# A layer norm that reads PSUM, in a kernel whose instruction order is packed by a scheduler: identity matmuls for the residual, a shorter GpSimd chain, a split second DFT

## The chip, the cores and the metric

The kernel runs on one core of one Trainium2 chip. The metric is the device time in microseconds (us) of one execution; each kernel is executed several times and the median is quoted. The profile is one such execution; its span is about 2 us shorter than the time (290.0 against 291.84 for before). In this kernel TensorE multiplies matrices, VectorE and ScalarE do elementwise work, GpSimd does small things and starts bulk loads, SyncE starts stores and small transposing transfers. Two memories are named below: PSUM, whose banks (`bank` in the profile) this kernel's matmuls write, and SBUF, which holds its other tiles.

A run over 1.5% above the fastest of its kernel is called slow, the others fast. Verdicts here use fast runs alone, with 2% as the bound of "faster" and "slower", and compare each kernel with the kernel before on the same chip in the same rounds.

## The reference, cut to what matters

Four batches of sorted block attention (8 heads, 768 tokens, head size 64) give `x` of 768 x 512 for each batch. Then:

```python
X = np.fft.fft(x, axis=1); X = np.fft.fft(X, axis=2)
u = x + np.real(X)
mu = u.mean(-1); var = ((u - mu) ** 2).mean(-1)
un = (u - mu) / np.sqrt(var + 1e-06)
out = u + np.maximum(un @ w_ch1, 0.0) @ w_ch2      # 512 -> 2048 -> 512
```

The kernel does the two Fourier transforms as matmuls with constant matrices ("first DFT" over tokens, "second DFT" over the 512 columns). A batch has six tiles of 128 tokens in two groups of three: group (b, 0) and group (b, 1). An MLP step works on one group. TensorE's MLP work fills most of the time; the attention of batch 0 must come first.

## The kernel before: the parts that matter

Every operation is handed to a planner with an estimated cost. The planner simulates the engines and emits one fixed order of instructions for each engine:

```python
            for s in o.succs:                  # after operation o was placed
                s.left -= 1
                for x in s.costs:
                    s.ready[x] = max(s.ready[x],
                                     o.end + (0.03 if x == e else self.XL))
```

So one changed cost or dependency can reorder everything behind it. The second DFT and the layer norm (`rt` holds x; `RSC` undoes a scale):

```python
    many("u", 6, [128, DM], F32)          # six result buffers in all
    # ... in dft2(b, g), tiles 0 to 2:
    for c in range(4):
        nc.tensor.matmul(ps[:, o:o + 256], y[:, c, w0:w0 + 128], dtab[:, c, :], ...)
    nc.tensor.matmul(ps, lt[:, l0:l0 + 128], rb, start=False, stop=True)
    V.scalar_tensor_tensor(u, rt[:, T, :], RSC, ps, op0=ALU.mult, op1=ALU.add)
    V.bn_stats(st, u)
    V.bn_aggr(mv[:, tt, :], st)
    # ... once for each group, G is GpSimd:
    G.tensor_scalar(var, var, 1e-6, None, op0=ALU.add)
    G.tensor_tensor(ny, var, mhalf, op=ALU.pow)
    G.tensor_tensor(nm, mean, ny, op=ALU.mult)
    G.tensor_scalar(nm, nm, -1.0, None, op0=ALU.mult)
    # ... each tile, on ScalarE or VectorE:
    un = u * ny + nm
    # batch 0: transposed by TensorE, copied, then the MLP
```

The result is added to `u`, and `u` is stored. The q and k of batches 2 and 3 are loaded late, into a buffer (`kq`) whose last readers are on VectorE:

```python
    def load_qk(nm, b, hf, prio):
        after = lns[1:2] if b > 1 else ()
        # ... gpsimd.dma_start into kq[:, slot[nm, b, hf], :]
```

The softmax here doesn't subtract the row's maximum and nothing guards it: scores larger than these inputs give would overflow.

## Time and profile before

| | before |
|---|---|
| time, median of 3 runs (range), us | 292.2 (292.06 to 293.51) |
| profiled span, us | 290.0 |
| first second-DFT matmul / first MLP matmul, us | 58.45 / 70.25 |
| TensorE busy in 120 to 150 and in 150 to 277, us | 30.00 of 30, 126.89 of 127 |

The page's picture of the run cuts the span in 40 slices (7.25 us each). Slices are counted from 0. A digit is the busy share in tenths; `PEclk` is the granted TensorE clock in tenths.

```profile
PE   0389988897999999999999999999999999999980
DVE  4697999999999999831579643145034226210020
PEclk9997999998899999999999999999999999999997
```

TensorE (`PE`) is nearly full from slice 10 on. VectorE (`DVE`) is full in slices 4 to 15, so there it is VectorE that limits. The table of stretches gives, for each stretch, its length, the busy time of TensorE, of its weight loads, of VectorE, ScalarE and GpSimd, then the granted clock, the DMA share and GB/s:

```profile
67.50:70.90 3.40, 1.64 (x21) 1.04 (x18) 3.33 (x12) 1.84 (x3) 1.87 (x5) 1.00 0.02 5
70.90:74.30 3.40, 3.40 (x17) 2.06 (x16) 2.89 (x6) 2.31 (x5) 3.39 (x6) 0.50 0.45 48
120.00:150.00 30.00, 30.00 (x222) 16.39 (x220) 14.24 (x34) 15.35 (x34) 5.86 (x9) 1.00 0.18 50
```

In 67.5 to 70.9 TensorE works less than half of the time (1.64 of 3.4 us), and in the next 3.4 us its clock is 0.50. A stretch of 3.4 us, as long as this one at half clock, is called a window below. The layer norm of the first group lies just ahead of that. The timeline of VectorE (start, duration, engine, line, operation, output and input, count):

```profile
59.77 1.87 DVE L1160 SCALAR_TENSOR_TENSOR u<-rt,bank 128x512 f32<-128x512 f16 x3
61.56 1.28 DVE L1186 BATCH_NORM_STATS2 st<-u 128x6 f32<-128x512 f32 x2
...
66.21 0.55 DVE L1217 TENSOR_SCALAR un<-u,ny,nm 128x512 f16<-128x512 f32 x1
```

and of TensorE (in brackets: idle time ahead, and what ended it):

```profile
58.45 0.60 PE L1149 MATMUL bank<-vcx,y 128*128 128x256 f16 x4 [0.34 <-ACT ex L961]
...
66.94 0.38 PE L1232 MATMUL bank<-pack,un 128*128 128x128 f16 x4 [0.15 <-DVE u L1181]
...
70.25 2.13 PE L1253 MATMUL bank<-ut,w1sb 128*128 128x384 f16 x8 [0.67 <-ACT ut L660]
```

From the second DFT (L1149) to the first transposes (L1232) pass 8.5 us, and TensorE fills most of them with attention work of batch 1.

```profile
109.39 0.34 SPq L1287 DMA_DIRECT2D out_dram<-u  x1
109.91 4.70 SPq L915 DMA_TRANSPOSE qt<-kq  x3
115.70 0.33 SPq L1289 DMA_DIRECT2D out_dram<-u  x1
```

### The profile page before, as it was taken

The numbers are of one execution on the slowest core, as the hardware profiler recorded it, in microseconds if no ns is written. First come the engines' busy times: TensorE is split into PE (matmuls) and PEld (weight loads), VectorE is DVE, ScalarE is ACT, GpSimd is POOL, SyncE is SP. The second block draws the span as 40 slices with busy tenths as digits, with TensorE's granted clock in tenths as the row PEclk, the third lists the DMA queues.
The fourth block names the chain that finished last, engine by engine and source line by source line (L and its number), as shares of the span: only waits on it lengthen the run. The fifth ranks groups of instructions, "written<-read, shape, count | busy, mean of one in ns | idle before, by whom it ended". The sixth has DMA issues, their size and how long they took to land.

```text
span 290.0 us, 5807 instructions
## 1 busy us (share of the span) xinstructions
PE 260.9 (90%) x2284; PEld 155.2 (54%) x2284; DVE 171.9 (59%) x405; ACT 157.9 (54%) x323; POOL 66.3 (23%) x104
## 2 busy tenths in 40 slices
PE   0389988897999999999999999999999999999980
PEld 0258866554565656554566456455555546545530
DVE  4697999999999999831579643145034226210020
ACT  2677979785778945970477037137415505425300
POOL 8973300015900640011220002032000212200021
PEclk9997999998899999999999999999999999999997
DMA  7999999910990897211113010311311111221001
GB/s 114 211 260 245 215 208 211 219 37 5 157 146 10 95 165 133 66 37 20 77 47 57 36 52 22 58 72 50 57 72 37 38 54 72 38 90 36 2 36 72
DMA packets 42529, 26.33 MB, mean 91 GB/s; under 512 B 30106, under 2 KB 38824, under 8 KB 42500
## 3 DMA queue, kind: packets, MB, share of 16 engines
q0 software_dynamic: 23536, 18.31, 37.4%
q1 hardware_dynamic: 18966, 7.64, 11.6%
q8 instruction: 18, 0.29, 0.4%
q14 instruction: 9, 0.07, 0.1%
HBM read 28.96 MB, written 6.29 MB: 122 GB/s over the span
## 4 chain that ended last, share of the span: by engine, by line
PE 62%; DVE 22%; DMA 8%; issue 3%; POOL 2%; ACT 1%; POOLq 0%; DVEq 0%
PE bank L1253 26%; PE bank L1274 25%; DMA hr<-in_v_dram 4%; DVE vsf L660 3%; DVE vcx L708 3%; DVE rt L1006 3%; DMA out_dram<-u,rows 2%; POOL kq L472 2%; DMA kq<-in_q_dram 2%; PE bank L1149 2%; PE bank L991 2%; DVE st L1186 1%; PE bank L952 1%; PE bank L897 1%; DVE ks L660 1%
## 5 line engine op out<-in xcount | busy, mean ns | idle before, releaser
L1265 ACT ACTIVATE hr<-bank 128x384 f16<-128x384 f32 x115 | 56.3, 491 | 75.2 <-PE bank L1253 74.4
L1253 PE MATMUL bank<-ut,w1sb 128*128 128x384 f16 x512 | 92.8, 329 | 0.7 <-ACT ut L660 0.7
L1274 PE MATMUL bank<-w2sb,hr 128*128 128x512 f16 x384 | 87.9, 379 | 0.0
L1253 PEld LDWEIGHTS <-w1sb 128*128 128x128 f16 x512 | 49.0, 99 | 34.8 <-issue 1.8
L1274 PEld LDWEIGHTS <-hr 128*128 128x128 f16 x384 | 36.7, 98 | 41.8 <-issue 0.2
L1282 DVE TENSOR_TENSOR u<-bank,u 128x512 f32<-128x512 f32 x24 | 16.5, 689 | 60.2 <-PE bank L1274 59.8
L961 ACT ACTIVATE ex<-bank 96x384 f32<-96x384 f32 x64 | 27.9, 485 | 6.3 <-PE bank L952 6.0
L1295 POOL DMA_INDIRECT out_dram<-u,rows x12 | 12.2, 1013 | 77.0 <-DVE u L1282 56.7
L1193 POOL TENSOR_SCALAR mv<-mv 128x3 f32<-128x3 f32 x8 | 1.9, 240 | 109.8 <-DVE mv L1188 109.8
L976 ACT ACTIVATE eb<-ex,negone 96x384 f16<-96x384 f32 x35 | 20.8, 615 | 0.2
L1213 ACT ACTIVATE un<-u,nm,ny 128x512 f16<-128x512 f32 x15 | 12.2, 810 | 11.8 <-DMA ut<-un 8.5
L1172 DVE SCALAR_TENSOR_TENSOR u<-rt,bank 128x510 f32<-128x510 f16 x12 | 8.1, 678 | 16.3 <-PE bank L1138 8.9
L991 PE MATMUL bank<-vsf,eb 97*128 97x65 f16 x416 | 16.5, 193 | 1.3 <-DVE rr L836 0.5
L1006 DVE TENSOR_TENSOR rt<-bank,rz 128x384 f16<-128x384 f32 x32 | 17.2, 549 | 0.3
L991 PEld LDWEIGHTS <-eb 97*128 97x128 f16 x416 | 15.4, 98 | 3.6 <-issue 1.3
L472 POOL DMA_DIRECT2D kq<-in_q_dram x20 | 16.4, 850 | 1.7 <-DMA kq<-in_q_dram 1.2
L1186 DVE BATCH_NORM_STATS2 st<-u 128x6 f32<-128x512 f32 x24 | 16.1, 686 | 0.3
L1160 DVE SCALAR_TENSOR_TENSOR u<-rt,bank 128x512 f32<-128x512 f16 x12 | 8.0, 684 | 13.9 <-PE bank L1153 13.5
L927 PE MATMUL bank<-pack,qr 128*128 128x128 f16 x48 | 4.8, 246 | 12.3 <-ACT qr L660 11.7
L724 PE MATMUL bank<-bdv,vcx 128*128 128x128 f16 (+1 forms) x128 | 12.6, 225 | 0.0
L952 PE MATMUL bank<-qt,ks 64*128 64x96 f16 x256 | 11.3, 207 | 1.3 <-DVE rt L1006 0.4
L897 PE MATMUL bank<-bdk,kq 128*64 128x128 f16 x192 | 10.7, 228 | 1.6 <-DVE bdk L636 0.8
(130 smaller groups left out, 338.2 us busy)
## 6 DMA issues: line engine op xcount, KB each, us to landing
kq<-in_k_dram POOLq DMA_DIRECT2D x8, 384.0 KB, 6.6
w1sb<-in_moe_w_ch_dram POOLq DMA_DIRECT2D x4, 512.0 KB, 16.0
w2sb<-in_moe_w_ch_dram POOLq DMA_DIRECT2D x4, 512.0 KB, 19.0
out_dram<-u SPq DMA_DIRECT2D x8, 256.0 KB, 2.0
kq<-in_q_dram POOLq DMA_DIRECT2D x4, 384.0 KB, 11.6
hr<-in_v_dram POOLq DMA_DIRECT2D x2, 768.0 KB, 11.2
kq<-in_v_dram POOLq DMA_DIRECT2D x2, 768.0 KB, 21.5
kq<-in_q_dram POOLq DMA_DIRECT2D x16, 96.0 KB, 5.5
```

What stands on the lines that cost most here:

```text
L472: o = P.add({eng: c}, lambda _: e.dma_start(dst, src), r=r, w=w, prio=prio, nbytes=nbytes, tag="load", after=after)
L897: nc.tensor.matmul(ps.ap[64 * h2:64 * h2 + 64, 128 * r3:128 * r3 + 128], k16[:, 2 * hl + h2, 3 * half + r3, :], bdk[:, 2 * hp + h2].rearra ...
L952: nc.tensor.matmul(pss[h2].ap[:, BLK * j:BLK * j + BLK], ks.ap[rows, 4 * g + j, :], qt.ap[rows, c0:c0 + BLK])
L961: nc.scalar.activation(ex.ap, pss[h2].ap[0:96, 0:384], AF.Exp, scale=SCALE),
L976: nc.scalar.activation(ed, src, AF.Identity, bias=negone[0:96])
L991: nc.tensor.matmul(po.ap[:, 65 * T:65 * T + 65], eb.ap[:, e0:e0 + 128], vsf[:, vi:vi + 65], start=(n == 0), stop=(n == len(WIN[T]) - 1), s ...
L1006: P.add({"DVE": (0.45, 0.56)}, lambda _: V.tensor_tensor(rt.ap[:, :, D * h:D * h + D], po3()[:, :, 0:D], rz.ap[:, :, None].broadcast_to([1 ...
L1186: P.add({"DVE": (0.6, 0.69)}, lambda _, u=u, st=st: V.bn_stats(st.ap, u.ap), r=[u], w=[st], tag="bn")
L1253: nc.tensor.matmul(ps.ap[:, 0:GT], w1sb[:, c, 128 * fc:128 * fc + 128], ut.ap[:, c, :], start=(c == 0), stop=(c == 3))
L1265: nc.scalar.activation(hr[g][:, fc, :], ps.ap[:, 0:GT], AF.Relu)
L1274: nc.tensor.matmul(ps.ap, hr[g][:, fc, 128 * tt:128 * tt + 128], w2sb[:, fc, :], start=(fc == 0), stop=(fc == 15))
L1282: V.tensor_tensor(u.ap, ps.ap, u.ap, op=ALU.add),
```

## The change

It shortens the chain of the first layer norm. In group (0, 0), x is added into PSUM by a matmul with a scaled identity; the statistics and the normalisation read PSUM; ScalarE copies the sum to `u` for later. In every group epsilon moves to VectorE and the bias chain on GpSimd shrinks. The second DFT is issued in two halves. The planner assumes that a result is ready sooner for the same engine. Core of the diff:

```diff
-    pack = ct("pack", [128, 240], F32)
+    pack = ct("pack", [128, 368], F32)          # + scaled identities, 64 KB more to load
+    rsi = pack[:, 240:368].bitcast(F16)
-    fq = ct("fq", [128, 2, 3, 128], F16)
+    fq = (a part of pmt, with the dependencies that this needs)
@@ planner
-                                     o.end + (0.03 if x == e else self.XL))
+                                     t + occ + 0.05
+                                     if x == e and x in ("DVE", "ACT")
+                                     else o.end + (0.03 if x == e
+                                                   else self.XL))
@@ dft2
-                    for c in range(4):           # four matmuls, then the last one
+                    for c in range(2):           # two; a second operation does c = 2, 3
...
+                    if xpe:                      # group (0, 0)
+                        xadd(ps, T, 0, False)    # identity matmul: adds x
@@ layer norm
+            if xpe:
+                P.add({"DVE": (0.6, 0.69)}, lambda _, ps=ps, st=st:
+                      V.bn_stats(st.ap, ps.ap), r=[ps], w=[st], tag="bn")
-        P.add({"POOL": (0.25, 0.25)}, lambda _: G.tensor_scalar(
+        P.add({"DVE": (0.07, 0.17)}, lambda _: V.tensor_scalar(
             mv.ap[:, :, 1], mv.ap[:, :, 1], 1e-6, None, op0=ALU.add),
-                    V.tensor_scalar(un.ap, u.ap, ny.ap[:, tt:tt + 1],
-                                    nm.ap[:, tt:tt + 1],
-                                    op0=ALU.mult, op1=ALU.add)
+                    V.tensor_scalar(dst, src, mv.ap[:, tt, 0:1],
+                                    ny.ap[:, tt:tt + 1],
+                                    op0=ALU.subtract, op1=ALU.mult)
@@ MLP: the last batch's groups swap places in the priorities
-            mlp(b, g, 100.0 + 10 * (2 * b + (g if b < B - 1 else 1 - g)), -300.0)
+            mlp(b, g, 100.0 + 10 * (2 * b + g), -300.0)
```

(cut: the copy to `u`, the subtracting identity for tiles 3 and 4, the remaining GpSimd lines)

More of the change, by code (lines that the diff above doesn't have):

```diff
@@ L115, in as32 @@
         return np.ascontiguousarray(m.astype(f16)).view(f32)
-    pack = np.concatenate([as32(np.eye(128)), as32(cm[:, 0:16]), cm,
-                           np.eye(128, dtype=f32)], axis=1)
+    eye = np.eye(128)
+    pack = np.concatenate([as32(eye), as32(cm[:, 0:16]), cm, eye.astype(f32),
+                           as32(RSC * np.concatenate([eye, -eye], axis=1))],
+                          axis=1)
     return dict(dtab=c(dtab, f16), cs=c(cs, f16), tab=c(tab, f32),
@@ L424 @@
     fo = ct("fo", [128, 2, 4, 128], F16)
-    fq = ct("fq", [128, 2, 3, 128], F16)
+    fq = pmt.rearrange("p t w -> p (t w)")[:, 0:768].rearrange(
+        "p (n t w) -> p n t w", n=2, w=128)
     many("y", 1, [128, 4, 2 * NK], F16)
@@ L548 @@
         pw=(pw, sort_net.rearrange("b h i j -> (b h) i j"), 8192),
-        pack=(pack, cn["pack"].ap(), 122880),
+        pack=(pack, cn["pack"].ap(), 188416),
         erow=(eb4[96:97], cn["erow"].ap().rearrange(
@@ L1076, in chain @@
             src = "eo" if ci < 0 else ("fo", ci) if ci < 2 else ("fq", ci - 2)
-            P.add(pe(mm(386, 3) + 0.04), f, r=[src, "cs"],
+            P.add(pe(mm(386, 3) + 0.04), f, r=[src, "cs"] + (
+                [("pm", 0, 0), ("pm", 0, 1), "pm2"] if ci > 1 else []),
                   w=[ps] + ([(y, ci, "a")] if ci >= 0 else ["lt96a"]),
@@ L1109, in dft1 @@
                 op=ALU.subtract if n == 0 else ALU.add),
-                r=["oo"], w=[("fq", n)], tag="fq")
+                r=["oo"], w=[("fq", n), ("pm", 0, 0), ("pm", 0, 1), "pm2"],
+                tag="fq")
         chain(2)
@@ L1133, in dft2, with xadd, f @@
             l0 = 128 * T if T < 3 else 384
+            xpe = b == 0 and g == 0
+            def xadd(ps, t, sign, stop):
+                nc.tensor.matmul(
+                    ps.ap.rearrange("p (n m) -> p n m", n=2),
+                    rsi[:, 128 * sign:128 * sign + 128],
+                    rt.ap[:, t, :].rearrange("p (m n) -> p n m", n=2),
+                    start=False, stop=stop, skip_group_check=True)
+            rts_ = [(rt, h) for h in range(H)]
             if T in (3, 4):
                 ps = banks_of[b, T - 3]
-                def f(_, ps=ps, T=T):
+                def f(_, ps=ps, T=T, b=b):
+                    if b == 0:
+                        xadd(ps, T - 3, 1, False)
                     nc.tensor.matmul(
@@ L1140, in f @@
                         rb, start=False, stop=True, skip_group_check=True)
-                P.add(pe(mm(512) + 0.03), f, r=lts, w=[ps, u], tag="dft2")
+                P.add(pe(mm(512, 2 if b == 0 else 1) + 0.03), f,
+                      r=lts + (rts_ + ["pack"] if b == 0 else []),
+                      w=[ps, u], tag="dft2")
             else:
@@ L1144, in dft2, with f @@
                 banks_of[b, T] = ps
-                def f(_, ps=ps, w0=w0, l0=l0):
-                    for c in range(4):
-                        o = 256 * (c % 2)
+                def f(_, ps=ps, w0=w0):
+                    for c in range(2):
                         nc.tensor.matmul(
-                            ps.ap[:, o:o + 256], y.ap[:, c, w0:w0 + 128],
-                            dtab[:, c, :], start=(c == 0), stop=False,
+                            ps.ap[:, 256 * c:256 * c + 256],
+                            y.ap[:, c, w0:w0 + 128], dtab[:, c, :],
+                            start=(c == 0), stop=False,
                             skip_group_check=True)
+                P.add(pe(mm(256, 2) + 0.03), f, r=ym[0:2] + ["dtab"],
+                      w=[ps, (u, "a")], tag="dft2")
+                def f(_, ps=ps, w0=w0, l0=l0, T=T):
+                    for c in range(2):
+                        nc.tensor.matmul(
+                            ps.ap[:, 256 * c:256 * c + 256],
+                            y.ap[:, 2 + c, w0:w0 + 128], dtab[:, 2 + c, :],
+                            start=False, stop=False, skip_group_check=True)
+                    if xpe:
+                        xadd(ps, T, 0, False)
                     nc.tensor.matmul(ps.ap, lt[:, l0:l0 + 128], rb,
@@ L1155, in f @@
                                      skip_group_check=True)
-                P.add(pe(mm(256, 4) + mm(512) + 0.05), f,
-                      r=ym + lts, w=[ps, u], tag="dft2")
-            if T < 3:
+                P.add(pe(mm(256, 2) + mm(512, 2 if xpe else 1) + 0.03), f,
+                      r=ym[2:4] + lts + (rts_ + ["pack"] if xpe else []),
+                      w=[ps, (u, "b")], tag="dft2")
+            if xpe:
+                P.add({"DVE": (0.6, 0.69)}, lambda _, ps=ps, st=st:
+                      V.bn_stats(st.ap, ps.ap), r=[ps], w=[st], tag="bn")
+            elif T < 3:
                 P.add({"DVE": (0.6, 0.69)}, lambda _, u=u, ps=ps, T=T:
@@ L1185, in dft2 @@
                       r=[ps] + [(rt, h) for h in range(H)], w=[u], tag="u")
-            P.add({"DVE": (0.6, 0.69)}, lambda _, u=u, st=st: V.bn_stats(
-                st.ap, u.ap), r=[u], w=[st], tag="bn")
+            if not xpe:
+                P.add({"DVE": (0.6, 0.69)}, lambda _, u=u, st=st: V.bn_stats(
+                    st.ap, u.ap), r=[u], w=[st], tag="bn")
             P.add({"DVE": (0.1, 0.17)}, lambda _, tt=tt, st=st: V.bn_aggr(
@@ L1191, in dft2 @@
         mvs = [(mv, tt) for tt in range(3)]
-        G = nc.gpsimd
-        P.add({"POOL": (0.25, 0.25)}, lambda _: G.tensor_scalar(
+        P.add({"DVE": (0.07, 0.17)}, lambda _: V.tensor_scalar(
             mv.ap[:, :, 1], mv.ap[:, :, 1], 1e-6, None, op0=ALU.add),
             r=mvs, w=[(mv, 3)], tag="ln")
-        P.add({"POOL": (0.9, 0.9)}, lambda _: G.tensor_tensor(
+        P.add({"POOL": (0.9, 0.9)}, lambda _: nc.gpsimd.tensor_tensor(
             ny.ap, mv.ap[:, :, 1], mhalf, op=ALU.pow),
             r=[(mv, 3), "mone"], w=[ny], tag="ln")
-        P.add({"POOL": (0.2, 0.2)}, lambda _: G.tensor_tensor(
-            nm.ap, mv.ap[:, :, 0], ny.ap, op=ALU.mult),
-            r=[(mv, 3), ny], w=[nm], tag="ln")
-        P.add({"POOL": (0.25, 0.25)}, lambda _: G.tensor_scalar(
-            nm.ap, nm.ap, -1.0, None, op0=ALU.mult), r=[nm], w=[(nm, 1)],
-            tag="ln")
         lns.append(P.ops[-1])
+        if (b, g) != (0, 0):
+            P.add({"DVE": (0.08, 0.18)}, lambda _: V.scalar_tensor_tensor(
+                nm.ap, mv.ap[:, :, 0], -1.0, ny.ap, op0=ALU.mult,
+                op1=ALU.mult), r=mvs + [ny], w=[nm], tag="ln")
         ut = Buf("ut")
@@ L1209, in dft2, with f @@
             un, pt, u = Buf("un"), Buf("pf"), us[b, g][tt]
-            def f(e, tt=tt, un=un, u=u):
+            ps = banks_of.get((b, tt))
+            def f(e, tt=tt, un=un, u=u, ps=ps):
+                dst, src = un.ap, u.ap
+                if (b, g) == (0, 0):
+                    dst = dst.rearrange("p (m n) -> p m n", n=2)
+                    src = ps.ap.rearrange("p (n m) -> p m n", n=2)
                 if e == "ACT":
-                    nc.scalar.activation(un.ap, u.ap, AF.Identity,
+                    nc.scalar.activation(dst, src, AF.Identity,
                                          scale=ny.ap[:, tt:tt + 1],
@@ L1216, in f @@
                 else:
-                    V.tensor_scalar(un.ap, u.ap, ny.ap[:, tt:tt + 1],
-                                    nm.ap[:, tt:tt + 1],
-                                    op0=ALU.mult, op1=ALU.add)
-            P.add({"ACT": (0.72, 0.81), "DVE": (0.45, 0.55)}, f,
-                  r=[u, ny, (nm, 1)], w=[un], tag="un")
+                    V.tensor_scalar(dst, src, mv.ap[:, tt, 0:1],
+                                    ny.ap[:, tt:tt + 1],
+                                    op0=ALU.subtract, op1=ALU.mult)
+            if (b, g) == (0, 0):
+                P.add({"DVE": (0.6, 0.7)}, f, r=[ps, ny] + mvs, w=[un],
+                      tag="un")
+                P.add({"ACT": (0.55, 0.65)}, lambda _, u=u, ps=ps:
+                      nc.scalar.copy(
+                          u.ap.rearrange("p (m n) -> p m n", n=2),
+                          ps.ap.rearrange("p (n m) -> p m n", n=2)),
+                      r=[ps], w=[u], tag="ucp", prio=P.prio + 0.5)
+            else:
+                P.add({"ACT": (0.72, 0.81), "DVE": (0.45, 0.55)}, f,
+                      r=[u, ny, nm] + mvs, w=[un], tag="un")
             if b > 0:
@@ L1347 @@
         for g in range(2):
-            mlp(b, g, 100.0 + 10 * (2 * b + (g if b < B - 1 else 1 - g)),
-                -300.0)
+            mlp(b, g, 100.0 + 10 * (2 * b + g), -300.0)
     with tc.manual_schedule():
```

## The prediction

> **What bounds the kernel now.** From about 75 us TensorE works without a gap: the table of stretches gives it 30.0 of 30 us busy in 120 to 150, 49.9 of 50 in 150 to 200, 77.0 of 77 in 200 to 277; two MLP matmul lines hold 51% of the chain of waits. Time can only be won where TensorE idles: at the start, in the attention and Fourier stage of batch 0 (about 6 us between 40 and 75), and in the tail after 277 (8.5 us: three indirect stores in series, 3.6 us each). In 30 to 50 VectorE is the limit (19.9 of 20 us busy, then 24.2 of 25 up to 75); the chain runs there from one VectorE instruction to the next.
>
> The change aims at the first layer norm. Second DFT begins at 58.45, first MLP matmul at 70.25. Between lie three x additions (0.66 us each), three statistics (0.65), four GpSimd instructions (64.33 to 66.17), normalisation and transposes. TensorE is busy only 1.64 of 3.4 us in 67.5 to 70.9, and in the next 3.4 us (70.9 to 74.3) the granted clock is 0.50. [...] It costs about 1.7 us.
>
> **What the change does.**
> - Removes three x additions on VectorE (2.0 us) in the first group, and three of four GpSimd instructions (about 0.9 us with hops) in each group.
> - Adds five 128x512 identity matmuls (0.215 us each: 1.1 us of TensorE), three PSUM copies on ScalarE (about 0.55 each), two VectorE instructions of about 0.15 per group. Normalisation in group 0 goes wholly to VectorE from PSUM: about 0.69 each (as PSUM-sourced adds take) against 0.55 from SBUF, three instead of one.
> - The split DFT changes no work; it lets half the matmuls run before the last y arrives.
> - The scheduler's new rule for same-engine results repacks everything. In the new order VectorE has, by this trace's durations, about 5.7 us less work ahead of the first transposed copy; TensorE has 42.5 us of work before the first MLP matmul (1.1 of it new) against 43.6.
> - 64 KB more constants ahead of the v load: up to 0.3 us.
> - The tail is unchanged: g=1 last in both, tile 0 finishing after 28 matmuls.
>
> **On the critical path.** I estimate last y about 1.5 us earlier, statistics done near 59, power near 60.4, third normalisation near 63, first MLP matmul near 66 instead of 70.25. TensorE has then done 2.2 us less of the old work, so net about 2.1 us. A filled gap probably (0.65) avoids the half clock: 1.1 us expected. Minus 0.3 for the load. All later layer norms are hidden behind MLP work: their shorter GpSimd part is worth nothing.
>
> **Predicted: 289.3 us**, 8 in 10 between 286.8 and 292.0. Faster by over 2%: 0.08; within 2%: 0.90; slower: 0.02.
>
> **What would show it.** First MLP matmul at 65 to 67; statistics on PSUM 0.65 to 0.70 us; normalisation from PSUM 0.65 to 0.72; no 0.5 clock near 70; TensorE still gapless from 80 to 277 less the gain; tail of 12 to 13 us after the last group's first addition.
>
> **What would make it wrong.** New waits from the repacked static order (TensorE behind VectorE or ScalarE in 75 to 110, where VectorE is 97% busy); half clock elsewhere; or more of the 6 us idle vanishing, which would give over 2%.

That a filled gap avoids the half clock is the estimate, from one window in the trace of before (1.64 of 3.4 us busy, then a clock of 0.50). 292.2, minus 2.1 for the work done earlier, minus 1.1 for the half clock (0.65 of 1.7), plus 0.3 for the load comes to 289.3. (The 0.3 agrees with 64 KB at the 217 GB/s that before moves in 10 to 20 us.)

## More of the kernel before

The program writes a `u` buffer again only when its store has landed.

The timelines of GpSimd and of SyncE show when the last loads are issued and when the first group's results are stored:

```profile
96.11 0.76 POOL L472 DMA_DIRECT2D kq<-in_k_dram  x1 [16.93 <-PE bank L724]
97.36 3.30 POOL L472 DMA_DIRECT2D kq<-in_q_dram  x4 [0.50 <-issue]
```

## The result, and the profile after

The changed kernel took 300.36 us (median of 4 runs, 299.46 to 300.44) against 292.69 (292.06 to 293.51, 4 runs) for the kernel before in the same rounds. The ratio is 1.0253, 95% interval 1.0217 to 1.0290: slower. Ratios in this document are the mean time of one kernel's fast runs over that of the other's of the same rounds, so they are not quite the ratio of the medians.

The prediction had given "slower" 2 chances in 100. The same views of the changed kernel, first the picture in slices (7.44 us each):

```profile
PE   0389989979999999699999999999999999999980
DVE  4597998879999999585359843235314315410020
PEclk9997995699999999799999999999999999999997
```

Two dips of the clock stand where before had none: slices 6 and 7, and slice 16. The table of stretches:

```profile
40.90:44.30 3.40, 2.26 (x37) 1.56 (x35) 3.40 (x13) 3.40 (x8) 0.00 (x0) 1.00 1.18 204
44.30:57.90 13.60, 13.47 (x166) 9.56 (x165) 11.54 (x35) 10.79 (x24) 0.00 (x0) 0.50 1.17 215
119.40:122.80 3.40, 0.72 (x12) 0.45 (x11) 1.26 (x3) 0.84 (x3) 0.00 (x0) 1.00 1.09 118
122.80:126.20 3.40, 3.40 (x19) 1.48 (x18) 2.75 (x9) 1.83 (x5) 0.87 (x1) 0.50 0.00 0
```

From 44.3 the clock is halved for 13.6 us, although TensorE is busy for 13.47 of them. At 119.4 TensorE nearly stops, and the next window is halved as well. The half clock at 70.9 is gone, as predicted, though in part by luck (see "Why the prediction was wrong"). The layer norm on VectorE, and the copies on ScalarE:

```profile
61.83 1.37 DVE L1194 BATCH_NORM_STATS2 st<-bank 128x6 f32<-128x512 f32 x2 [0.15 <-ACT u L1264]
...
65.29 1.53 DVE L1257 TENSOR_SCALAR un<-bank,mv,ny 128x512 f16<-128x512 f32 x2 [0.40 <-POOL ny L1233]
...
67.33 0.81 DVE L1257 TENSOR_SCALAR un<-bank,mv,ny 128x512 f16<-128x512 f32 x1
```

```profile
61.21 1.91 ACT L1264 COPY u<-bank 128x512 f32<-128x512 f32 x3 [0.28 <-PE bank L1186]
```

and TensorE:

```profile
59.30 0.82 PE L1170 MATMUL bank<-vcx,y 128*128 128x256 f16 x6
...
66.16 0.39 PE L1146 MATMUL bank<-rt,pack 128*128 128x512 f16 x1 [1.13 <-DVE un L1257]
...
71.97 0.82 PE L1302 MATMUL bank<-ut,w1sb 128*128 128x384 f16 x4
```

The second DFT began 0.85 us later than before (59.30 against 58.45). The chain from there to the first normalisation was shorter (6.0 us against 7.8). The first MLP matmul still came later (71.97), because the new order puts batch 1's attention in front of it, not because it waited: between 68 and 80 TensorE is idle for 0.14 us, where before had 1.48. (Over the whole stage, 56 to 80, it is 2.26 against 2.54.)

The groups of waits of TensorE between 56 and 130 us (in total, times, longest):

```profile
PE bank L959 <- DVE u L1197: 2.7, 1, 2.7
PE bank L1146 <- DVE un L1257: 1.1, 1, 1.1
```

The first of these is the stop at 119. The chain of waits says what it hangs on:

```profile
114.86 0.51 SPq L1339
...
115.42 6.00 DMA out_dram<-u
...
121.54 0.70 DVE u L1197
...
122.28 0.33 PE bank L959 x7
```

A store whose issue ended at 115.4 landed after 6.00 us; in the kernel before, the same store took about 3.1. VectorE had to wait for it, since it writes the same `u` buffer, and TensorE waited behind VectorE. The GpSimd timeline shows what was on the way at that time:

```profile
106.02 0.76 POOL L479 DMA_DIRECT2D kq<-in_k_dram  x1 [23.92 <-issue]
107.65 3.29 POOL L479 DMA_DIRECT2D kq<-in_q_dram  x4 [0.87 <-PE bank L1323]
```

The last batch's loads, issued at 96.1 to 104.7 before, are now issued at 106.0 to 115.0 and land until 121.3. Their buffer is read last by VectorE (`vcx`), which now finishes at 106.9 instead of 99.0.

To place the loss I added up, for both traces, the time that the matmuls need at full clock, and asked how much later the changed kernel reaches the same sum. (Identity matmuls and fillers of the experiments are left out. For one matmul I used 0.4167 ns for each column + 2.5 ns, which fits the traces of before and after: at full clock, matmuls of 128, 256, 384 and 512 columns follow one another after 56, 109, 162 and 216 ns, in the median.) Call this the lag. It is an estimate; counted in slightly different ways, its points move by up to 0.25 us:

| stretch of before, us | lag at its end, us | change |
|---|---|---|
| start to 28 | 0.74 | +0.74 |
| 28 to 56 (attention) | 3.34 | +2.60 |
| 56 to 80 (second DFT, layer norm) | 2.14 | -1.20 |
| 80 to 116 | 2.60 | +0.46 |
| 116 to 124 (store wait, half clock) | 7.14 | +4.54 |
| 124 to the end | 7.66 | +0.52 |

The aim of the change, the stretch of 56 to 80, did gain 1.2 us, though that is hardly more than what before's half clock at 70.9 had cost there (0.8 to 1.1, under best1). All of the loss lies elsewhere.

### The profile page after: what moved, and what is told of

Same layout as the page of the kernel before. It is cut to its first block, busy times and chain, and to the rows that moved or that the text cites. A ratio compares the mean times of both kernels' runs of the same rounds, so it can differ in the third digit from the quotient of the medians.

```text
span 297.6 us, 5785 instructions
## 1 busy us (share of the span) xinstructions
PE 267.7 (90%) x2289; PEld 157.0 (53%) x2289; DVE 175.4 (59%) x422; ACT 155.5 (52%) x321; POOL 60.1 (20%) x80
## 4 chain that ended last, share of the span: by engine, by line
PE 70%; DVE 15%; DMA 8%; issue 3%; POOL 1%; POOLq 0%; ACT 0%; SPq 0%; DVEq 0%
PE bank L1323 27%; PE bank L1302 26%; DMA hr<-in_v_dram 5%; PE bank L998 4%; PE bank L904 3%; PE bank L959 2%; DMA out_dram<-u 2%; PE bank L1070 2%; DVE rt L1013 2%; DMA out_dram<-u,rows 2%; DVE vsf L667 2%; PE bank L731 1%; PE bank L1170 1%; PE bank L1180 1%; PE bank L1186 1%
## 5 line engine op out<-in xcount | busy, mean ns | idle before, releaser
L1302 PE MATMUL bank<-ut,w1sb 128*128 128x384 f16 x512 | 94.0, 329 | 0.2
L1314 ACT ACTIVATE hr<-bank 128x384 f16<-128x384 f32 x109 | 53.5, 491 | 77.8 <-PE bank L1302 77.4
L1233 POOL TENSOR_TENSOR ny<-mv,mhalf 128x3 f32<-128x3 f32 x8 | 7.1, 884 | 110.1 <-DVE mv L1230 110.1
L998 PE MATMUL bank<-vsf,eb 97*128 97x65 f16 x416 | 18.7, 203 | 1.1 <-DVE rr L843 0.4
L998 PEld LDWEIGHTS <-eb 97*128 97x128 f16 x416 | 17.0, 104 | 3.3 <-issue 1.3
L1197 DVE SCALAR_TENSOR_TENSOR u<-rt,bank 128x512 f32<-128x512 f16 x9 | 6.0, 681 | 18.1 <-PE bank L1186 15.2
L959 PE MATMUL bank<-qt,ks 64*128 64x96 f16 x256 | 12.7, 219 | 3.6 <-DVE u L1197 2.7
L1224 DVE BATCH_NORM_STATS2 st<-u 128x6 f32<-128x512 f32 x21 | 14.3, 691 | 0.5
L667 ACT CAST vsf<-bank 96x512 f16<-96x512 f32 x16 | 11.6, 793 | 5.2 <-PE bank L731 5.1
L959 PEld LDWEIGHTS <-ks 64*128 64x128 f16 x256 | 7.3, 100 | 11.9 <-issue 11.0
```

Source lines behind the costliest of these rows:

```text
L667: (nc.scalar.copy if e == "ACT" else V.tensor_copy)(dst, src)
L959: nc.tensor.matmul(pss[h2].ap[:, BLK * j:BLK * j + BLK], ks.ap[rows, 4 * g + j, :], qt.ap[rows, c0:c0 + BLK])
L998: nc.tensor.matmul(po.ap[:, 65 * T:65 * T + 65], eb.ap[:, e0:e0 + 128], vsf[:, vi:vi + 65], start=(n == 0), stop=(n == len(WIN[T]) - 1), s ...
L1302: nc.tensor.matmul(ps.ap[:, 0:GT], w1sb[:, c, 128 * fc:128 * fc + 128], ut.ap[:, c, :], start=(c == 0), stop=(c == 3))
L1314: nc.scalar.activation(hr[g][:, fc, :], ps.ap[:, 0:GT], AF.Relu)
```

## The experiments

My theory after reading the traces had three losses: (S) 64 KB of constants ahead of the first loads, (C) half clock in the attention stage, because the new order leaves a thin window there, and (W) late loads that slow a store on which a result buffer waits. Rivals: the planner's new rule is a bad rule (A); the new order costs time in itself (O); the new layer norm gains nothing (N).

A difficulty has to be told first. In the profiles of before and after TensorE starts at half speed: up to 16 us its matmuls of 512 columns come every 0.427 us, later, at full clock, every 0.216 (medians). The first window at full speed begins at 16.3 us in the profile of before and at 17.0 in after, but at 28.4, 30.4, 30.5 and 31.2 in four of the other profiles. Nearly the same order is then about 3 us behind (lag at 28 us: 3.82 in after_rsi, below, against 0.74 in after; that is 1.0% of the span, though a part of it need not be the clock). In the 12 profiles without dummy matmuls at the start, not all of one order, the first full window began anywhere from 15.8 to 31.2 us. It widens the scatter of several runs below.

### after_oldrule: is the planner's rule to blame?

```diff
@@ after, planner only
-                                     t + occ + 0.05 if x == e and x in ("DVE", "ACT") else ...
+                                     o.end + (0.03 if x == e else self.XL))
```

> The changed kernel with the scheduler's old rule for results on the same engine; everything else of the change stays. If the repacked order is what loses (theory A: the new rule packs VectorE and ScalarE differently, TensorE falls to the half clock in 44 to 58 and waits for a store at 119), the half clock before 60 us and the 2.7 us wait near 119 both go, and the time is 290 to 294 us. If the layer norm parts themselves lose (theory B: PSUM reads, identity matmuls), it stays at 298 to 301 us.

Measured: 303.78 us (303.27 to 305.99), ratio 1.0406. The change with the old rule is slower still, outside both ranges that I had given. Its profile has half clock at 44.1 to 54.3, 64.5 to 67.9 and 149.9 to 160.1, and 3.3 us of TensorE waiting for `u`. A is refuted as the whole cause: without the new rule, another new order shows the same two kinds of loss in other places.

### before_newrule: the rule alone

The converse: before, with only the planner's new rule.

```diff
@@ before, planner only
-                                     o.end + (0.03 if x == e else self.XL))
+                                     t + occ + 0.05 if x == e and x in ("DVE", "ACT") else ...
```

> The kernel before with only the scheduler's new rule. Theory A: it loses too, 296 to 301 us, with a half clock stretch in the attention stage. Theory B: 291 to 294 us, like the kernel before.

Measured: the fast runs give 1.0033 (0.9996 to 1.0069), but of six runs three were slow: 293.22, 293.77, 295.8, 298.24, 299.66, 300.72. The profile fell on the slowest: half clock at 47.4 and at 119.1, and TensorE waited 2.9 us for `u`, with the last loads issued at 107.5 to 116. In the fast runs the rule alone costs nothing clear of noise. The profile of a slow run shows the same two kinds of loss, but what the rule alone costs in them stays open.

### after_warm: fill the thin window

Six matmuls into unused columns ahead of each batch-0 scores group, so that TensorE is less idle there.

```diff
+                if b == 0:
+                    for n in range(6):
+                        nc.tensor.matmul(pss[n % 2].ap[:, 384:512], idh, idh)
```

> The changed kernel with six 128x128 matmuls on constants ahead of each scores group of batch 0, into unused columns of the same bank; the order of all else is untouched. If the low activity of TensorE in 40.9 to 44.3 us is what brings the half clock of 44.3 to 57.9, and that clock costs what the progress curves say (3.0 us lag gained in 40 to 56), the half clock goes and the time falls by 2.5 to 4 us, to 296.5 to 298. If the half clock is only a symptom of an attention stage limited by VectorE and ScalarE, the time changes by less than 1 us.

Measured: 298.03 us (297.05 to 298.93), ratio 1.018 (1.0140 to 1.0221, unclear against the 2%). The half clock at 44 is gone:

```profile
PEclk9995999997999999999999999999999999999996
```

The lag from 28 to 56 went from 3.08 to 3.15, so the 2.60 us of this stretch vanished. Part was given back at the start (lag 3.08 at 28, half clock from 22.1 for two windows), and part in the next stretch: a half clock now stands at 66.5 to 69.9 (slice 9), and 56 to 80 no longer gains its 1.2 us. On the other hand the store wait (116 to 124) cost 2.6 instead of 4.5. C is shown as a cause: between 32 and 60 us all four profiles of the change without these fillers (after, after_oldrule, after_ubuf, after_rsi) have a half clock, and none of the six with them (after_warm, all3, all3_oldln, pin, pin_oldln, best2). Its size is about 2.6 us in its own stretch and only about 1.4 by 80 us; what it is worth in the end was not measured alone. Useless matmuls made the kernel faster (ratio 1.0180 against the change's 1.0253).

### after_ubuf: take away what the store wait waits for

One of the `u` buffers is placed in memory that is dead by then; the order is unchanged.

```diff
+        us[1, 0][2].ap = tab.rearrange("p a b c -> p (a b c)")[:, 0:DM]
```

> The changed kernel in the same order, but the third u tile of batch 1, first group, lies in the table of the row sums, which is dead by then, instead of the buffer whose store lands at 121.3 us. If that wait is the cause of the lag that jumps from 2.6 to 7.0 us at 119 us (2.7 us of waiting and 1.7 us of half clock in the window after it), the wait and the half clock of 122.8 to 126.2 go and the time falls by 4 to 5 us, to 295.5 to 296.5. If another wait stands behind it, less than 2 us.

Measured: 295.04 us (294.05 to 296.03), ratio 1.0088, which is 1.6% under the changed kernel's 1.0253. The store is as late as ever (landed at 121.84), but nobody waits for it: the lag is 2.46 at 116 and 2.55 at 124, and no half clock follows. The loss by this wait is shown: about 4.5 us in the trace, 4.8 by the ratios. That the late loads are what slows the store is taken up under before_late18.

### after_rsi: load the 64 KB later

```diff
-    rsi = pack[:, 240:368].bitcast(F16)
+    rsi = ct("rsi", [128, 256], F16)      # own load, issued after that of "tab"
```

> The changed kernel in the same order, with the 64 KB of identity constants in a load of their own, issued after the last early loads instead of ahead of q, k and v. If those 64 KB are what makes q, k and v of batch 0 land 0.8 us later (v at 17.14 instead of 16.35 us), v lands at 16.3 to 16.5 again and the time falls by 0.5 to 1 us, to 299.4 to 299.9. If the shift of the start is chance, nothing changes.

Measured: 300.22 us (298.85 to 303.12), ratio 1.0263. The q load landed at 8.87 instead of 9.77 and the lag at 16 us fell from 0.78 to 0.09, so S is real at the start. The total did not move: in the profiled run, the slowest of five, the clock was not at full speed until 30.5. The 0.7 us are smaller than what the start's clock does by chance.

### all3 and all3_oldln: everything repaired, with the new and with the old layer norm

All3 joins the last three edits. All3_oldln keeps all3's order of the planned operations (the planner still sees the new ones), but what is emitted for group (0, 0)'s norm is the old way:

```diff
@@ all3_oldln against all3
-                    if xpe:
-                        xadd(ps, T, 0, False)
-                      V.bn_stats(st.ap, ps.ap)
+                    V.scalar_tensor_tensor(u, rt[:, T, :], RSC, ps, ...)
+                    V.bn_stats(st.ap, u.ap)
-                      nc.scalar.copy(u, ps)
+                      None
@@ and epsilon and the bias chain on GpSimd, un = u * ny + nm
```

> The changed kernel in the same order with all three mends: warm scores, other u buffer, constants late. If the three losses are separate and add up (2.3, 5.3 and 0.7 us against 300.4), 291.5 to 293, level with the kernel before. If one hides another, 293.5 to 296.

> As all3, in the same order, but the first group's layer norm as in the kernel before: x added on VectorE, statistics and normalisation from SBUF, four GpSimd instructions, no identity matmuls. Theory L (the layer norm part is worth what the prediction says, 2 us less its 1.1 us of matmuls and whatever clock it keeps): slower than all3 by 1 to 2.5 us. Theory N (the gap is filled with other matmuls and nothing is won): within 0.7 us of all3.

Measured: all3 298.56 us (295.68 to 300.14), ratio 1.0135; all3_oldln 297.97 (293.71 to 300.96), ratio 1.0069. One of all3's four runs and two of all3_oldln's, its profile among them, were slow. My expectation of 291.5 to 293 for all3 was missed. Its lag was already 4.34 at 24 us (full clock only from 28.4), and another store (issued at 109.3, landed at 115.5) now held a `u` buffer: VectorE wrote it only at 115.6, after 2.0 us of idling, and TensorE later waited 1.6 us behind VectorE. The pair's times scatter by 5 to 7 us and say nothing about the layer norm. A better controlled pair was needed.

### before_tail: the tail, as a side path

Before's last three stores run one after the other (2.7 to 2.9 us each). This version finishes the last group's tiles one by one, so that the first store starts earlier.

```diff
+                c = mm(512, 4)
+                P.add({"PE": (c, c - 0.03)} if (b, g) == (B - 1, 1) else pe(c), f,
```

> The kernel before with the last group's second MLP matmuls tile by tile instead of two tiles in turn, all else in the same order. The first of its three indirect stores, which follow one another, can start 12 matmuls (2.6 us) earlier: 289 to 290.5 us instead of 292.2, if the chain of stores is what ends last. No gain if the last tile's matmuls end the run.

Measured: 290.94 us (288.13 to 292.7, one of them slow), ratio 0.9962. In its profile the first of the three stores starts at 274.54 instead of 278.22, and the span is 286.3. Its profile also had a half clock in the attention stage (43.9 to 54.1), in the *old* order; it cost 1.3 us of lag there. So the old order is not safe from C, only further from it.

### pin and pin_oldln: the layer norm alone, under control

Two `u` buffers in dead memory, and 87 dummy matmuls ahead of and between the first TensorE operations, meant to bring the clock up early in every run. In both profiles it was full at 6.0 us, half again from 9.4 to 16.2, and full from 26.4 up to the layer norm. Otherwise all3 and all3_oldln.

```diff
+        for n in range(2):
+            us[1, 0][1 + n].ap = tab...[:, DM * n:DM * n + DM]
+        warm = [45, 16, 8, 8, 10]
         for o in order:
+            if o.eng == "PE" and warm:
+                for n in range(warm.pop(0)):
+                    nc.tensor.matmul(banks[0][:, 384:512], idh, idh)
             o.fn(o.eng)
```

> The changed kernel with all three repairs (idle-column matmuls before the batch-0 scores, the 64 KB constants loaded late, and now two result buffers moved into dead memory) and with 87 extra 128x128 matmuls ahead of and between the first TensorE operations, so that the clock is at full speed from the start in every execution. Theory (the loss is made of start, clock in attention and store wait; the layer norm itself gains): first full clock before 14 us, no wait of TensorE for a result buffer at 110 to 122, and 289 to 292 us, that is 0 to 1% under the kernel before. Rival (the repacked order costs time in itself, whatever the clock and the stores): 294 or more although no half clock lies before 60 and no wait at 110 to 122. The spread of its times should also be smaller than that of the version without the extra matmuls (295.7 to 300.1).

> The same order and the same pinned start as the run before it, but the first group's layer norm done the old way (x added by VectorE, scaled bias, epsilon on GpSimd, no identity matmuls). The difference of the two is the layer norm part of the change alone. Theory: 3 to 4 us slower than the run before it (the order that was fixed without the pin lagged by 4.0 more over 60 to 80, of which about 1.7 was a half clock), so 292 to 296. Rival (the layer norm part gains nothing, since the kernel waits elsewhere later on): within 1 us of it.

Measured: pin 294.07 us (293.15 to 294.88), ratio 1.0050 (1.0017 to 1.0084); pin_oldln 296.74 (295.64 to 297.72), ratio 1.0152 (1.0116 to 1.0189). The ranges no longer overlap. The new layer norm is worth 2.67 us between the medians, 1.0050 / 1.0152 = 0.990 or 3.0 us by the ratios, and 2.2 us between the two profiled spans. N is refuted. TensorE's waits show where, first pin, then pin_oldln:

```profile
PE bank L1156 <- DVE un L1267: 1.1, 1, 1.1
```

```profile
PE bank L1302 <- DVE un L1277: 4.2, 1, 4.2
```

The same order waits 4.2 us for the old normalisation and 1.1 us for the new one. (The 4.2 us are followed by one more window of half clock: 63.9 to 70.8 in pin_oldln, 64.0 to 67.4 in pin.) This is the worth of the new norm in an order that was planned for it. What it would be worth in an order planned for the old one was not run. But pin stayed above the 289 to 292 that I expected: with these repairs, the change is still not faster than before. That points to O.

### before_pin: does the new order cost time in itself?

Before, with the 87 dummy matmuls only.

```diff
@@ before
+        warm = [45, 16, 8, 8, 10]
+            if o.eng == "PE" and warm: ...     # as in pin
```

> The kernel before with only the 87 extra matmuls at the start, as in the fully repaired changed kernel. With it, that kernel (294.07) and its old-layer-norm twin (296.74) can be compared at equal start. Theory: about 292.5, since the start phase of the kernel before was already good and its half clock at 70.9 stays; then the repacked order costs about 4 us against the old order before the layer norm gives 2.7 back, part of it the longer half clock at 64. Rival (the new order costs nothing once clock and stores are repaired): 296 or more.

Measured: 293.97 us (292.95 to 297.1), ratio 1.0050 (1.0008 to 1.0092). I had expected about 292.5, but the dummies cost the old order 0.7 to 0.8 us at the start, and its profile has a half clock at 46.6 to 56.8 that cost another 1.3; the one at 70.9, which I had expected to stay, was absent. By the ratios, pin equals before_pin, and pin_oldln is 1.0152 / 1.0050 = 1.010 of it, 3 us more. So O is right in this sense: with these repairs, the new order with the old norm is about 3 us slower than the old order, and the new norm gives those 3 us back. The profiles show the place. Between 56 and 80 us TensorE is idle for 2.54 us in before, 2.80 in before_pin, 4.86 in pin_oldln and 2.30 in pin. With the old norm put into it, the new order has less other TensorE work ready beside the first layer norm; with the new norm it idles about as much as the old order does. An order that the new rule plans for the old norm (before_newrule's fast runs) cost nothing clear of noise, so the 3 us are likely those of the old norm in an order made for another, and not of any new order. What else they contain is not settled (pin also carries 48 fillers in the attention), and the two ratios come from two chips.

### before_lateload and before_late18: bring the late loads into the old order

Clears of dead memory on GpSimd, ahead of the last batch's loads: eight in the first run, eighteen in the second.

```diff
+            if o.tag == "load" and o.n >= b3_loads and not held:
+                held = 1
+                for n in range(18):          # 8 in before_lateload
+                    nc.gpsimd.memset(tab..., 0.0)
             o.fn(o.eng)
```

> The kernel before with one thing added: eight GpSimd clears of dead memory (about 1 us each by estimate) ahead of the last batch's q and k loads, so that these loads are issued about 8 us later and meet the stores of the first MLP group. Theory (late loads delay the stores that free the result buffers): the stores of the first group land at 119 to 122 instead of 115.7 to 116.6, a wait of TensorE behind VectorE for a result buffer of 1 to 3 us at 112 to 121, and 1 to 5 us more than the kernel before. Rival (the wait came from the changed order of TensorE, not from the loads): no such wait and the same time within 0.5 us.

Measured: 292.62 us, ratio 1.0000 (0.9966 to 1.0033). This experiment failed: the clears ran in idle time at 88 to 96 and the loads were issued at 96.8, hardly later than before. It tests nothing.

> The kernel before with eighteen GpSimd clears of dead memory (1.02 us each, measured in the run with eight) ahead of the last batch's q and k loads. They start at 88 and end at about 106, so the ten loads are issued at 106 to 115, as in the changed kernel, instead of 96 to 105. Theory (late loads delay the stores that free the result buffers): the stores issued at 109.4 and 115.7 land 2 to 3 us later, VectorE waits for the first or the second of them before its result writes at 113.1 and 120.7, TensorE waits behind it 1 to 3 us between 113 and 124, and the run is 0.5 to 4 us over the kernel before. Rival (the wait came from the new order of TensorE alone): no such wait, same time within 0.5 us.

Measured: 299.3 us (297.86 to 302.39, one of six slow), ratio 1.0236 (1.0195 to 1.0278, unclear against the 2%), more than the 0.5 to 4 us that I had expected. The loads now go out as late as in the changed kernel, first in its GpSimd timeline, and TensorE waits, in its groups of waits:

```profile
87.03 18.45 POOL L1358 MEMSET tab<- 128x1028 f32 x18 [7.97 <-PE bank L813]
105.43 0.76 POOL L472 DMA_DIRECT2D kq<-in_k_dram  x1
106.21 3.29 POOL L472 DMA_DIRECT2D kq<-in_q_dram  x4
```

```profile
PE bank L952 <- DMA qt<-kq: 3.7, 1, 3.7
```

The old order with late loads loses as much as the whole change did. The victim is another one than I had written: not a store but a small transposing transfer, issued at 114.69, which landed after 7.49 us instead of 2.76, and of which TensorE needs the result. The stores suffered only indirectly: SyncE, which issues both, reached the store at 121.16 instead of 115.70, and VectorE waited 0.8 us for a buffer. The lag rose from 0.42 at 116 to 6.02 at 120, and a half clock followed at 121.6. So the general form of W is shown: in these traces small transfers under way together with the bulk loads took two to three times as long as in a quieter stretch (6.00 us against 2.03 to 3.1 for a store, 7.49 against 2.76 for a transposing one), and whoever needs one of them in that time waits. Which one it is depends on the order.

### best1 and best2: the repairs without the change, and with it

Best1 is before_tail with the dummy matmuls at the start, ten ahead of each of the first group's later two transposed tiles and eight ahead of the first MLP matmul. Best2 is pin with the same tail and twenty dummies at 62 us.

```diff
@@ best1 against before_tail, besides the 87 at the start
+                if g == 0 and tt > 0:
+                    for n in range(10):
+                        nc.tensor.matmul(pt.ap[:, 384:512], idh, idh)
+                    if (b, g, fc) == (0, 0, 0):
+                        for n in range(8):
+                            nc.tensor.matmul(ps.ap[:, 384:512], idh, idh)
@@ best2 against pin, besides the tail
+                    if bt == (0, 5):           # batch 0, tile 5, second DFT
+                        for n in range(8): ...
+            if b == 1 and fill:                # batch 1's next product with v
+                for n in range(12): ...
```

> The kernel before with the last group's second product tile by tile, the same extra matmuls at the start, ten idle-column matmuls before the first group's transposes and eight before its first product, against the half clock at 70.9. Theory [...]: full clock from 14 to the end of the work, and 286 to 289 us, 1 to 2% under the kernel before. Rival (the half clock at 70 doesn't come from TensorE's low activity): half clock near 70 as before and about 290.5.

> The fully repaired changed kernel with two things more: the last group's second product tile by tile, and twenty idle-column matmuls at 62 (its window from 60.6 to 64.0 had 45% of its clock cycles streaming columns, and the next window was at half clock). Theory: no half clock at 64 (1.7 us) and a tail shorter by about 2.6 us: 289 to 291, equal to the repaired kernel before (289.72) within 1.5 us. Rival (half clock at 64 comes from elsewhere): half clock at 64 stays and 291.5 or more.

(The 45% come from pin's timeline: the matmuls from 60.61 to 64.0 have 3661 columns, at 0.4167 ns each 1.53 of 3.4 us.)

Measured: best1 289.72 us (288.72 to 291.54), ratio 0.9915 (0.9876 to 0.9954), above the 286 to 289 that I expected. Best2 291.48 (291.12 to 292.21), ratio 0.9943 (0.9919 to 0.9967), just above the expected 289 to 291. In best1 the window in question is at full clock (table of stretches):

```profile
68.40:71.80 3.40, 2.53 (x53) 2.44 (x50) 3.40 (x12) 1.60 (x3) 1.52 (x4) 1.00 0.00 0
```

Its lag to before fell from 1.45 at 72 us to 0.33 at 76, so before's half clock at 70.9 had cost about 1.1. But before_tail and before_pin, which have no fillers in this place, were at full clock there too (their lag fell by 0.8), so it is not shown that the fillers did it. In best2 the half clock at 64 went as well, but that brought little: from 28 to 76 us its lag fell by 0.45 where pin's fell by 0.17, and at the end it was 2.82 against pin's 2.37, because its start was 0.75 behind pin's. So by the traces best2's gain over pin comes from the tail. Best1 is the fastest version, 0.85% under before, and does not contain the change.

## Why the prediction was wrong

**The step that failed** is the assumption behind the sum: that outside the layer norm everything stays as it is ("The scheduler's new rule for same-engine results repacks everything", and then no term for it except a gain). I had even listed "new waits from the repacked static order" and "half clock elsewhere" as what could go wrong, and gave a slower kernel 2 chances in 100. The attention stage was expected 1.5 us earlier and came later: the second DFT began at 59.30 us instead of 58.45. The runs put in its place:

- *Half clock in the attention stage*: no term in the prediction; +2.6 us of lag in its stretch; gone with fillers (after_warm).
- *A transfer slowed by late loads*: no term, with "TensorE still gapless from 80 to 277"; +4.5 us; gone with a spare buffer (after_ubuf), and a loss of the same kind appears in the old order with late loads (before_late18).
- *64 KB more constants*: "up to 0.3 us"; measured 0.74 at the start, 0.09 with the load moved (after_rsi).

**What was right.** The direction of the layer norm part: its chain became shorter (6.0 us against 7.8). Statistics on PSUM took 0.67 to 0.70 us (predicted 0.65 to 0.70). The tail stayed.

**What agrees in part by luck.** I expected 2.1 us plus 1.1 us for the avoided half clock; in a fixed order the new norm is worth 2.2 to 3.0 (pin against pin_oldln), but that order was planned for the new norm, while my sum was made against the old order. The half clock at 70.9 went, but it was absent in two profiles of the old order too (before_tail, before_pin), and wherever fillers removed the one in the attention stage without more fillers at 62, one came back at 64 to 69 (after_warm 66.5, all3 65.9, pin 64.0).

**What was mis-sized inside it.**
- Normalisation from PSUM took 0.80 to 0.81 us, not 0.65 to 0.72; from SBUF it takes 0.55. The new instruction differs in its source and also reads its columns in another order, and no run separates the two.
- I let ScalarE's copies run beside VectorE's statistics. In the trace they take turns on each bank: copies 61.21 to 63.12, statistics 61.83 to 63.86, and VectorE's idle time ahead of the first is ended by the copy. It cost little: a copy takes 0.59 us, but VectorE was busy with other work until 61.67, idled for 0.15 us before the first statistics and not at all between the three.
- The times of the chain: statistics done at 63.9 instead of near 59, third normalisation at 68.1 instead of near 63, because the stage began 0.85 us later and not about 1.5 earlier, and the chain from there took longer than I had summed.
- First MLP matmul at 65 to 67: it came at 71.97 with no idle TensorE before it. It was a bad yardstick, since the planner may put other useful work there; the lag is a better one.

**Where the expected gain went.** With start, stores and attention repaired, new norm and new order together are level with the old kernel (pin against before_pin). One can split this into a gain of 2.2 to 3.0 us by the norm and a loss of about 3 us by an order that has less other TensorE work beside it (pin_oldln), but the split rests on an old norm in an order not made for it. On top came start, clock and transfers: 0.74 + 2.60 + 4.54 = 7.9 us of lag. The other rows of the lag table add up to -0.2, and the two profiled spans differ by 7.6.

## What to carry to other kernels

Where a scheduler fixes the order, a local change is a new kernel: before predicting, compare the new order stage by stage, above all when bulk loads are released and which small transfers they will meet. Measure the local part with the order held fixed and the start of the clock pinned, or chance will hide it. A thin stretch of TensorE work cost twice here, once by its gap and once by the half clock behind it (2.7 us of waiting at 119, then 3.4 us at a clock of 0.50); but test first whether TensorE is what the stretch waits for: in best2, filling it gained 0.3 us at most. The parts of the change outside the first layer norm (the swapped priorities, the shorter GpSimd chain of later groups, `fq`'s new place) were not run alone.
